# Attention and FFN in one kernel: x loaded into eight tiles of a pool of five, K made chunk by chunk, GpSimd's clearings moved

## The chip, the cores and the metric

The kernel runs on one core of a Trainium2 chip. A core has five engines with an instruction stream each: TensorE (PE: matrix products, its weight loads are shown apart as PEld), VectorE (DVE), ScalarE (ACT), GpSimd (POOL) and SyncE (SP, which here only issues DMAs). Each engine works through its own stream in order and waits on semaphores for the others. The metric is the time of one execution on the device in microseconds (us), lower is better.

## The reference

One token sequence x of 2048 x 512 goes two ways, and a gate mixes them. Way A is attention with 32 heads of 16 numbers, where all heads share one K and one V (multi-query). Way B is a feed-forward layer of width 1792 with SiLU.

```python
g = sigmoid((x * gate_w).sum(-1, keepdims=True))
q = (x @ wq) as 32 heads of 16;  k = x @ wk;  v = x @ wv      # wk, wv: 512 x 16
p = softmax(q @ k.T * 16 ** -0.5)                              # 32 x 2048 x 2048
a = (p @ v, heads side by side) @ wo
b = silu(x @ w1) @ w2                                          # 512 -> 1792 -> 512
out = g * a + (1 - g) * b
```

All is in float32. The kernel gets that precision from 16-bit parts: an operand is split into a high part and the rest, and a product is three matmuls (high x high, high x rest, rest x high).

## The kernel before

**Prologue (`first_pass`, L432 to L567).** It brings x in, turns it over and makes the first operands of the attention, before the first score.

- `loads` (L301) issues on SP's queue eight DMAs of 256 tokens of x, into four tiles of 512 tokens (a chunk), each with its own buffer. The loads of `wqr` (two of wq's four column blocks) stand behind the second DMA of x. The two first pieces of w1 (`raw`) follow on the same queue. wk, wv and the gate's weights come over ACT's queue.
- `T(c, t)` (L328, L331) turns 128 tokens of chunk c on PE (four transposes into a PSUM buffer `pt`, of which there are four). `split` (L121 to L124) takes the high half out on ACT and the rest on DVE, into `xs`. A buffer is free for the next T when DVE is through.
- `wkv` holds wk, wv and the gate's weights side by side. GpSimd gathers it, and `split` makes its two halves `wkvs` (ACT, then DVE).
- `W` (L485) makes wq's halves, on ACT and GpSimd, for two of the four blocks of 128 rows at a time. `Q(kt)` (L502) is a fourth of the product that gives q for the first 512 tokens.
- `K(t)` (L493, L498) is 48 matmuls of 128 columns: for tokens 128 t to 128 t + 127 of **each of the four chunks**, one chunk in each group of 32 partitions. So it needs x of all four chunks. Three K's write `pk`, the fourth another bank `mi`.
- From K come `kh` (the halves of K, on ACT L525 and L530, on DVE L536) and a bound on K's size (`absmax` L523, the minimum against a mask `mxa` L524, the product `prep` L532, `kv_`, `kab` L534). From q come `qs_` and `qa`; `q_bound` (L423) multiplies `qa` by `kab` and gives the shift `s1`, `place` (L348) puts K's first chunk into `KT`, and two groups of matmuls (L554, L558) put q and the shifts into `qb`, the operand of the first scores.
- `cleared(VP, VF)` and `cleared(nus, sc)` (L217) are GpSimd's clearings of V's two buffers, some constants and the second `qb`. The first stands ahead of the gathering of `wkv`, the second behind W(2).

**Main phase (`attention`, L785).** 16 rounds (4 chunks of queries x 4 blocks of 8 heads), each of 32 steps of 64 keys. A step has two score groups (`S`, L1140, 8 matmuls each), two exponentials of 128 x 1024 on ACT (L1146), and its share of P times V (`pv`, L1157, L1166). That share comes in one of two kinds. The whole kind multiplies float32 P by float32 V in one go (8 matmuls `P,VF`). The split kind multiplies P's upper 16 bits by V (part A, `P,VP`) and then P's rest (part B, `L,VP` or `raw,VP`), which DVE has to make first with two subtractions (L1152). The FFN and the projections are fed in as passes (L826): a pass is 4 matmuls, or 8 where two outputs share the array. V itself is made in `begin` (L1172, L1190) while the first scores run.

The order of all this is not found at run time. A planner (`advance`, L1466) steps through PE, ACT and DVE with fixed lengths for every piece of work (`PASS`, `WHOLE`, `EXP`, `LOW` at L30 and L31) and writes each engine's stream in the order that comes out. `decide` (L1309) picks the kind of a step by the time that DVE has left, and `pe_next` (L1370) the next piece on PE.

**End (L1489 to L1520).** Behind the last score PE finishes P times V of the last steps and the last FFN product (`pm<-xs,w1s`). Its tanh (ACT L857), the SiLU (DVE L860), a cast by DMA (POOL L870) and a subtraction (DVE L874) give the last `H`, and 24 matmuls of full width (L830), four last projections (L1518) and the stores close the kernel.

## Time and profile before

| what | us |
|---|---|
| median of 3 runs (lowest, highest) | 1043.51 (1042.72, 1044.07) |
| the profiled execution | 1041.77 |
| its span | 1040.0 |
| first score on PE, first exponential on ACT | 27.14, 27.94 |
| last score on PE | 1013.17 |
| last tanh on ACT | 1018.35 |

The span is what the hardware profiler recorded between the first and the last instruction; 1.8 us of the execution lie around it. In the lines of the profile a row is start, length, engine, line, operation, output<-inputs, count, and in brackets the idle time ahead of it with what ended it. "x48" are 48 instructions that overlap in a row's length. A matmul of float32 makes two records.

### The profile page before, as it was taken

The numbers are of one execution on the slowest core, as the hardware profiler recorded it, in microseconds if no ns is written. First come the engines' busy times: TensorE is split into PE (matmuls) and PEld (weight loads), VectorE is DVE, ScalarE is ACT, GpSimd is POOL, SyncE is SP. The second block draws the span as 40 slices with busy tenths as digits, with TensorE's granted clock in tenths as the row PEclk, the third lists the DMA queues.
The fourth block names the chain that finished last, engine by engine and source line by source line (L and its number), as shares of the span: only waits on it lengthen the run. The fifth ranks groups of instructions, "written<-read, shape, count | busy, mean of one in ns | idle before, by whom it ended". The sixth has DMA issues, their size and how long they took to land.

```text
span 1040.0 us, 63947 instructions
## 1 busy us (share of the span) xinstructions
PE 1012.4 (97%) x30021; PEld 559.1 (54%) x30021; DVE 927.5 (89%) x1197; ACT 993.7 (96%) x1109; POOL 62.4 (6%) x141
## 2 busy tenths in 40 slices
PE   8999999999999999999999999999999999999996
PEld 6335555555555555565555555555555555555552
DVE  7778887779999999999999998999899989999984
ACT  5999999999999999999999999999999999999990
POOL 5001111110000000000000000000000000000000
PEclk9999999999999999999999999999999999999998
DMA  5123221311010121111101021110110021110001
GB/s 206 43 81 73 80 65 50 80 44 30 14 32 12 39 50 20 30 19 31 18 14 30 10 70 24 28 22 14 46 25 14 10 63 21 25 19 14 9 4 49
DMA packets 28091, 39.77 MB, mean 38 GB/s; under 512 B 5689, under 2 KB 19370, under 8 KB 27818
## 3 DMA queue, kind: packets, MB, share of 16 engines
q0 software_dynamic: 10656, 15.73, 7.3%
q1 hardware_dynamic: 16442, 19.27, 6.0%
q8 instruction: 237, 3.88, 1.6%
q10 hardware_dynamic: 720, 0.59, 0.2%
q14 instruction: 36, 0.29, 0.1%
HBM read 19.98 MB, written 8.25 MB: 27 GB/s over the span
## 4 chain that ended last, share of the span: by engine, by line
PE 55%; ACT 33%; DVE 5%; issue 5%; DMA 1%; SPq 0%; ACTq 0%; DVEq 0%
ACT P L1146 31%; PE pm L826 20%; PE pv L1166 17%; PE S L1140 14%; ACT e L857 2%; DVE L L1152 2%; DVE e L860 1%; DVE raw L1152 1%; PE pm L830 1%; PE S L830 1%; DMA xn<-in_A_x_dram 1%; PE pt L331 1%; DVE acc L807 0%; DVE T L1081 0%; DMA H<-e 0%
## 5 line engine op out<-in xcount | busy, mean ns | idle before, releaser
L1146 ACT ACTIVATE P<-S 128x1024 f32<-128x1024 f32 x1024 | 960.3, 1068 | 9.4 <-PE pv L1166 3.3
L1140 PE MATMUL S<-qb,KT 50*32 50x512 f16 x8192 | 444.2, 379 | 10.6 <-ACT P L1146 8.9
L1152 DVE TENSOR_TENSOR L<-P 128x1024 f16<-128x1024 f32 x318 | 379.5, 1217 | 31.1 <-ACT P L1146 30.3
L1140 PEld LDWEIGHTS <-KT 50*32 50x32 f16 x8192 | 200.1, 89 | 250.1 <-issue 162.7
L826 PE MATMUL pm<-xs,w1s 64*32 64x512 f16 x5376 | 305.6, 375 | 0.7 <-DVE e L860 0.3
L826 PE MATMUL pm<-w2s,H 64*32 64x512 f16 x5184 | 293.6, 375 | 1.2 <-DVE e L860 0.7
L1166 PE MATMUL pv<-P,VF 64*32 64x512 f32 x4224 | 284.0, 589 | 0.0
L1152 DVE TENSOR_TENSOR raw<-P 128x1024 f16<-128x1024 f32 x178 | 212.4, 1216 | 5.8 <-ACT P L1146 5.5
L826 PEld LDWEIGHTS <-w1s 64*32 64x32 f16 x5376 | 132.0, 92 | 54.2 <-issue 9.9
L826 PEld LDWEIGHTS <-H 64*32 64x32 f16 x5184 | 127.3, 93 | 48.6 <-issue 10.1
L1166 PE MATMUL pv<-P,VP 64*32 64x512 bf16 x1984 | 112.4, 386 | 0.0
L1166 PEld LDWEIGHTS pv<-P,VF 64*32 64x32 f32 x4224 | 83.0, 106 | 25.7 <-issue 3.8
L1166 PEld LDWEIGHTS <-VP 64*32 64x32 f16 x3968 | 71.0, 92 | 35.9 <-issue 8.9
L1166 PE MATMUL pv<-L,VP 64*32 64x512 f16 x1272 | 86.9, 376 | 0.1
L826 PE MATMUL pm<-xs,wqs 64*32 64x512 f16 x1152 | 86.0, 375 | 0.7 <-DVE e L860 0.7
L870 POOL DMA_DIRECT2D H<-e x56 | 29.8, 532 | 798.8 <-DVE e L860 757.5
L826 PE MATMUL pm<-wo_s,O 64*32 64x512 f16 x1440 | 66.9, 375 | 0.1
L1166 PE MATMUL pv<-raw,VP 64*32 64x512 f16 x712 | 55.8, 376 | 0.0
L860 DVE SCALAR_TENSOR_TENSOR e<-e,pm 128x512 f32<-128x512 f32 x56 | 38.3, 684 | 11.0 <-ACT e L857 10.7
L807 DVE SCALAR_TENSOR_TENSOR acc<-pm,g,acc 128x512 f32<-128x512 f32 x48 | 35.7, 746 | 9.0 <-PE pm L826 8.1
L826 PEld LDWEIGHTS <-wqs 64*32 64x32 f16 x1152 | 37.3, 92 | 9.4 <-issue 2.6
L874 DVE TENSOR_TENSOR H<-e,H 128x512 f16<-128x512 f32 x56 | 38.2, 682 | 3.7 <-DMA H<-e 3.7
(202 smaller groups left out, 491.3 us busy)
## 6 DMA issues: line engine op xcount, KB each, us to landing
H<-e POOLq DMA_DIRECT2D x56, 128.0 KB, 2.3
raw<-in_B_w_dram POOLq DMA_DIRECT2D x24, 256.0 KB, 3.0
qb<-qd SPq DMA_DIRECT2D x180, 32.0 KB
xn<-in_A_x_dram SPq DMA_DIRECT2D x8, 512.0 KB
out_dram<-acc SPq DMA_DIRECT2D x14, 256.0 KB
qd<-qx SPq DMA_DIRECT2D x13, 256.0 KB
raw<-in_A_wo_dram POOLq DMA_DIRECT2D x4, 256.0 KB, 3.0
qb<-sh SPq DMA_DIRECT2D x60, 2.0 KB
```

Source lines behind the costliest of these rows:

```text
L331: nc.tensor.transpose(pt[:, kt], xn[c].rearrange("p t (d k) -> p t k d", k=KD)[:, t, kt], ident)
L807: nc.vector.scalar_tensor_tensor(a, po, gate[:, m:m + 1], a, op0=OP.mult, op1=OP.add)
L826: nc.tensor.matmul(self.bank[32 * m:32 * m + 32], l(i, rows, 32 * m), r(j, rows), start=first, stop=last)
L830: nc.tensor.matmul(self.bank, l(i, slice(0, 128), 0, 128), r(j, slice(0, 128)), start=first, stop=last)
L857: nc.scalar.activation(e, o.bank, AF.Tanh, scale=t_scale)
L860: nc.vector.scalar_tensor_tensor(e, e, 1.0, o.bank, op0=OP.add, op1=OP.mult)
L870: nc.gpsimd.dma_start(H[:, 0], e)
L874: nc.vector.tensor_tensor(H[:, 1], e, H[:, 0], op=OP.subtract)
L1140: nc.tensor.matmul(sc[32 * m:32 * m + 32, f], KT[b:b + 50, k0:k0 + 32], qtile[i][b:b + 50, m // 2, j], start=True, stop=True)
L1146: nc.scalar.activation(probs[s][:, 2 * j:2 * j + 2], banks.pop(p), AF.Exp, scale=scale_of(*rounds[steps[s][0]]))
L1152: nc.vector.tensor_tensor(lows[s, j], probs[s][:, js], upper(probs[s])[:, js], op=OP.subtract)
L1166: nc.tensor.matmul(pvs[i][h][32 * j:32 * j + 32], a[r], b[r], start=k == 0 and n != "B", stop=k == NK - 1 and n != "A")
```

## The change

x comes into eight tiles of 256 tokens out of a pool of five buffers, so that the sixth, seventh and eighth load wait until PE has turned the first, second and third tile. The load of `wqr` moves behind the fourth tile of x. `W(n)` works on 128 columns of all four row blocks, so that Q needs only W(0).

`K(c)` now takes **one chunk's** four groups of 128 tokens, one in each group of partitions, and so can run as soon as that chunk is turned. The keys then stand in another order in `KT`, and V and the gate are made in the same order (L1190, L1207: the operand is read as four blocks of 128 columns). The halves of `wkv` are made early by ACT and GpSimd and not by DVE. All of GpSimd's clearings stand behind W(1). Behind K the order on ACT, DVE and PE changes, and K's first chunk is put into `KT` by DVE and not by ACT.

In the planner the constant `WHOLE` = 0.866 is gone. `HALF` = 0.435 is there, and the whole kind (now "W") counts as 2 x 0.435 = 0.870. The two half kinds "N" and "M" that `pv` knows are given to no step.

```diff
-PASS, PASS_S, PASS_P, WHOLE, LATE = 0.217, 0.219, 0.231, 0.866, 0.23
+PASS, PASS_S, PASS_P, HALF, LATE = 0.217, 0.219, 0.231, 0.435, 0.23
...
-    def loads(sb, q_cols, wq_at=NCH - 1):
+    def loads(sb, q_cols, wq_at=NCH - 1, ahead=2 * NCH):
...
-        for c in range(NCH):
-            t_ = sb.tile([128, 4, D], F32, name=f"xn{c}")
-            if c == wq_at:
+        for n in range(2 * NCH):
+            t_ = sb.tile([128, 2, D], F32, name="xn", bufs=ahead)
+            nc.sync.dma_start(t_, x[n * 256:n * 256 + 256].rearrange("(t p) d -> p t d", p=128))
+            xn.append(t_)
+            if n == 2 * wq_at + 1:
                 nc.sync.dma_start(wqr, by_row(wq)[:, :, :q_cols])
-            for a in range(2):
-                nc.sync.dma_start(t_[:, 2 * a:2 * a + 2], x[c * 512 + a * 256:c * 512 + a * 256 + 256].rearrange("(t p) d -> p t d", p=128))
-            xn.append(t_)
...
-            nc.tensor.transpose(pt[:, kt], xn[c].rearrange("p t (d k) -> p t k d", k=KD)[:, t, kt], ident)
+            nc.tensor.transpose(pt[:, kt], xn[2 * c + t // 2].rearrange("p t (d k) -> p t k d", k=KD)[:, t % 2, kt], ident)
...
-            xn, wqr, wkv, gather = loads(sb, 256, 1)
+            xn, wqr, wkv, gather = loads(sb, 256, 1, 5)
...
-            def W(kt):
-                nc.scalar.activation(wqs[:, 0, kt:kt + 2, 0:256], wqr[:, kt:kt + 2], AF.Copy, scale=SQ)
-                nc.gpsimd.tensor_scalar(wqr[:, kt:kt + 2], wqr[:, kt:kt + 2], SQ, None, op0=OP.mult)
-                nc.gpsimd.tensor_tensor(wqs[:, 1, kt:kt + 2, 0:256], wqr[:, kt:kt + 2], wqs[:, 0, kt:kt + 2, 0:256], op=OP.subtract)
+            def W(n):
+                b = slice(128 * n, 128 * n + 128)
+                nc.scalar.activation(wqs[:, 0, :, b], wqr[:, :, b], AF.Copy, scale=SQ)
+                nc.gpsimd.tensor_scalar(wqr[:, :, b], wqr[:, :, b], SQ, None, op0=OP.mult)
+                nc.gpsimd.tensor_tensor(wqs[:, 1, :, b], wqr[:, :, b], wqs[:, 0, :, b], op=OP.subtract)
...
-            def K(*ts):
-                for t in ts:
+            def K(c):
+                out = pk[c // 3][:, c % 3 * 128:c % 3 * 128 + 128]
+                for n, (i, j) in enumerate(((0, 0), (1, 0), (0, 1))):
                     for kt in range(KD):
-                        for n, (i, j) in enumerate(PARTS):
-                            for c in range(NCH):
-                                nc.tensor.matmul(pk[t // 3][32 * c:32 * c + 32, t % 3 * 128:t % 3 * 128 + 128], wkvs[:, i, kt, 0:32],
-                                                 xs[:, j, kt, c * 512 + t * 128:c * 512 + t * 128 + 128],
-                                                 start=kt + n == 0, stop=kt == KD - 1 and n == 2)
+                        for g in range(4):
+                            nc.tensor.matmul(out[32 * g:32 * g + 32], wkvs[:, i, kt, 0:32],
+                                             xs[:, j, kt, c * 512 + g * 128:c * 512 + g * 128 + 128],
+                                             start=kt + n == 0, stop=kt == KD - 1 and n == 2)
...
+            first, last = slice(0, 384), slice(384, 512)
+
+            def largest(n, bank):
+                absmax(mx[:, n:n + 1], bank)
+                nc.vector.tensor_scalar(mxa[:, n], m_k, mx[:, n:n + 1], None, op0=OP.min)
+
+            def rest(b, r):
+                nc.vector.scalar_tensor_tensor(kh[1][:, r], b, k_to, kh[0][:, r], op0=OP.mult, op1=OP.subtract)
...
             place_masks()
             row_masks()
-            cleared(VP, VF)
             gather()
-            T(0, 0, 1, 2, 3)
+            nc.gpsimd.tensor_scalar(wkv, wkv, SKV, None, op0=OP.mult)
+            T(0, 0, 1)
+            nc.scalar.activation(wkvs[:, 0], wkv, AF.Copy)
+            nc.gpsimd.tensor_tensor(wkvs[:, 1], wkv, wkvs[:, 0], op=OP.subtract)
+            T(0, 2, 3)
             T(1, 0, 1)
             W(0)
             T(1, 2, 3)
-            W(2)
+            T(2, 0)
+            K(0)
+            T(2, 1)
+            W(1)
+            cleared(VP, VF)
             cleared(nus, sc)
-            T(2, 0)
-            split(wkvs[:, 0], wkvs[:, 1], wkv, SKV)
-            T(2, 1, 2)
+            T(2, 2, 3)
+            K(1)
+            T(3, 0, 1, 2)
+            K(2)
+            nc.scalar.activation(kh[0][:, first], pk[0][:, first], AF.Copy, scale=k_to)
+            T(3, 3)
+            largest(0, pk[0][:, first])
             Q(0)
-            T(2, 3)
-            T(3, 0, 1, 2, 3)
             Q(1)
-            K(0, 1, 2)
-            absmax(mx[:, 0:1], pk[0][:, 0:384])
-            nc.vector.tensor_scalar(mxa[:, 0], m_k, mx[:, 0:1], None, op0=OP.min)
-            nc.scalar.activation(kh[0][:, 0:384], pk[0][:, 0:384], AF.Copy, scale=k_to)
             K(3)
             Q(2)
-            absmax(mx[:, 1:2], pk[1][:, 0:128])
-            nc.vector.tensor_scalar(mxa[:, 1], m_k, mx[:, 1:2], None, op0=OP.min)
-            nc.scalar.activation(kh[0][:, 384:512], pk[1][:, 0:128], AF.Copy, scale=k_to)
+            Q(3)
+            nc.scalar.activation(kh[0][:, last], pk[1][:, 0:128], AF.Copy, scale=k_to)
+            nc.scalar.activation(qs_[:, 0], pq, AF.Copy, scale=qsc)
+            largest(1, pk[1][:, 0:128])
             prep = misc()
             nc.tensor.matmul(prep[:, 0:8], flat(sel_k), flat(mxa), start=True, stop=True)
-            nc.vector.tensor_reduce(kv_, prep[:, 0:8], axis=AX.X, op=OP.max)
-            nc.vector.tensor_scalar(kab, hmask, kv_, k_to * 2.0 ** -10 * (1 + 2.0 ** -9), op0=OP.mult, op1=OP.mult)
-            for b, r in enumerate((slice(0, 384), slice(384, 512))):
-                nc.vector.scalar_tensor_tensor(kh[1][:, r], pk[b][:, 0:r.stop - r.start], k_to, kh[0][:, r], op0=OP.mult, op1=OP.subtract)
-            Q(3)
-            pieces_.step(by_scalar=True)
-            qs_ = wk_.tile([128, 2, 512], F16, name="qs_")
-            qa = wk_.tile([128, 512], F16, name="qa")
-            nc.scalar.activation(qs_[:, 0], pq, AF.Copy, scale=qsc)
-            nc.vector.tensor_scalar(qa.bitcast(U16), qs_[:, 0].bitcast(U16), 0x7FFF, None, op0=OP.bitwise_and)
-            nc.vector.scalar_tensor_tensor(qs_[:, 1], pq, qsc, qs_[:, 0], op0=OP.mult, op1=OP.subtract)
-            place(misc(), 0, True)
-            pu = misc()
-            q_bound(pu, qa)
-            s1 = wk_.tile([64, 512], F16, name="s1")
-            nc.scalar.activation(s1, pu[0:64], AF.Copy, scale=-2.0 ** 10 / ONE, bias=SHIFT * LAM / ONE)
...
-            for n in range(2):
+
...
+            spread(0)
+            rest(pk[0][:, first], first)
+            nc.vector.tensor_reduce(kv_, prep[:, 0:8], axis=AX.X, op=OP.max)
+            nc.vector.tensor_scalar(kab, hmask, kv_, k_to * 2.0 ** -10 * (1 + 2.0 ** -9), op0=OP.mult, op1=OP.mult)
+            rest(pk[1][:, 0:128], last)
+            nc.vector.tensor_scalar(qa.bitcast(U16), qs_[:, 0].bitcast(U16), 0x7FFF, None, op0=OP.bitwise_and)
+            pu = misc()
+            q_bound(pu, qa)
+            pieces_.step(by_scalar=True)
+            nc.scalar.activation(s1, pu[0:64], AF.Copy, scale=-2.0 ** 10 / ONE, bias=SHIFT * LAM / ONE)
+            nc.vector.scalar_tensor_tensor(qs_[:, 1], pq, qsc, qs_[:, 0], op0=OP.mult, op1=OP.subtract)
+            place(misc(), 0, False)()
+            spread(1)
...
-            if k == 0:
+            if k == 0 and n != "M":
                 pvs[i] = [pO.tile([128, 512], F32, name=f"pv{h}") for h in range(2)]
-            a = VF[:, k] if n == "N" else VP[:, k]
+            a = VF[:, k] if n in "WNM" else VP[:, k]
+            q = slice(0, 256) if n == "N" else slice(256, 512) if n == "M" else slice(0, 512)
             for j in range(4):
-                b = upper(probs[s])[:, j] if n == "A" else probs[s][:, j] if n == "N" else lows[s, j // 2][:, j % 2]
+                b = upper(probs[s])[:, j] if n == "A" else probs[s][:, j] if n in "WNM" else lows[s, j // 2][:, j % 2]
                 for h, r in enumerate((lo, hi_)):
-                    nc.tensor.matmul(pvs[i][h][32 * j:32 * j + 32], a[r], b[r], start=k == 0 and n != "B", stop=k == NK - 1 and n != "A")
-            if n != "A":
+                    nc.tensor.matmul(pvs[i][h][32 * j:32 * j + 32, q], a[r], b[r, q], start=k == 0 and n != "B", stop=k == NK - 1 and n != "A")
+            if n in "BMW":
                 probs.pop(s)
...
-                        nc.tensor.matmul(v[32 * c:32 * c + 32], wkvs[:, i, kt, 32:64], xs[:, j, kt, c * 512:c * 512 + 512],
+                        nc.tensor.matmul(v[32 * c:32 * c + 32], wkvs[:, i, kt, 32:64], xs[:, j, kt].rearrange("p (c g n) -> p g c n", c=NCH, g=4)[:, c],
...
-                        z = gz.rearrange("p (c u o) -> p u c o", c=NCH, o=1)[h, 2 * a:2 * a + 2]
+                        z = gz.rearrange("p (u c o) -> p u c o", c=NCH, o=1)[h, 2 * a:2 * a + 2]
...
-                    how[s] = "N"
+                    how[s] = "W"
...
-                if r is not None and (left_of[s][0] != "N" or max(r, now["PE"]) <= most):
+                if r is not None and (left_of[s][0] in "AB" or max(r, now["PE"]) <= most):
...
-            length = {"A": PASS_P, "B": PASS, "N": WHOLE}[n]
+            length = {"A": PASS_P, "B": PASS, "N": HALF, "M": HALF, "W": 2 * HALF}[n]
...
-            x = pv_next(end - PASS_S - LATE - WHOLE + SLACK if p < 2 * len(steps) else 1e9)
+            x = pv_next(end - PASS_S - LATE - 2 * HALF + SLACK if p < 2 * len(steps) else 1e9)
```

The last of it moves the streams of the main phase. They are alike up to the 60th score group. Then they differ in detail: 261 steps are of the whole kind (264 before) and 251 of the split kind (248 before), and DVE gets 502 subtractions L1152 (496 before).

On PE, in the prologue, the products for K (`pk`, `mi`, from `xs` and the weights in `wo_s`) stand behind the last transposes (`pt`) and behind two of the four Q's (`pq`). Before:

```order
L442 MATMUL mi<-ident 128x128 x15
L331 MATMUL pt<-ident,xn_187 128x128 x16
L331 MATMUL pt<-ident,xn_190 128x128 x16
L331 MATMUL pt<-ident,xn_194 128x128 x12
L132 MATMUL pq<-xs,wqs 128x512
...
L331 MATMUL pt<-ident,xn_197 128x128 x16
...
L498 MATMUL pk<-xs,wo_s 32x128
```

And after, where each row of L498 stands for the first of 48:

```order
L441 MATMUL mi<-ident 128x128 x15
L330 MATMUL pt<-ident,xn 128x128 x36
L498 MATMUL pk<-xs,wo_s 32x128
...
L330 MATMUL pt<-ident,xn 128x128 x12
...
L330 MATMUL pt<-ident,xn 128x128 x4
L132 MATMUL pq<-xs,wqs 128x512
...
L498 MATMUL mi<-xs,wo_s 32x128
```

K(0) moved up behind the ninth T, K(1) and K(2) behind the twelfth and the fifteenth. All four Q's stand behind the last T, two ahead of K(3) and two behind it.

On GpSimd (POOL) in the prologue the clearings of `VP` and `VF` stand ahead of the gathering of `wkv`. Before:

```order
L461 MEMSET sels__215 64x512
L219 MEMSET VP 128x1024
L219 MEMSET VF 128x1024
L322 COPY wkv<-wkr 128x4x16
L324 COPY wkv<-gwr 128x4
L487 TENSOR_SCALAR wqr<-wqr 128x512
L488 TENSOR_TENSOR wqs<-wqr,wqs 128x2x256
L219 MEMSET nus 128x48
```

After:

```order
L460 MEMSET sels__219 64x512
L321 COPY wkv<-wkr 128x4x16
L323 COPY wkv<-gwr 128x4
L521 TENSOR_SCALAR wkv<-wkv 128x256
L524 TENSOR_TENSOR wo_s<-wkv,wo_s 128x256
L487 TENSOR_SCALAR wqr<-wqr 128x4x128
L488 TENSOR_TENSOR wqs<-wqr,wqs 128x4x128
L219 MEMSET VP 128x1024
L219 MEMSET VF 128x1024
L219 MEMSET nus 128x48
```

The two clearings moved from the front of the stream to behind both W's, right ahead of the constants `nus` and the clearing of `qb`, and the two rows on `wkv` are new on this engine.

On PE, at the end of the main phase, from the last score group (`S`) on, with the FFN's passes (`pm`) and P times V (`pv0`). Before:

```order
L1140 MATMUL S_33004<-qb1_84,KT_60 32x512
L826 MATMUL pm_32807<-xs_66,w1s_67 32x512
L1166 MATMUL pv0_31190<-P_32859,VF_63 32x512
...
L1166 MATMUL pv0_31190<-P_32931,VF_63 32x512
...
L1166 MATMUL pv0_31190<-P_32994,VF_63 32x512
...
L830 MATMUL S_33097<-w2s_68,H_31485 128x512
```

After:

```order
L1158 MATMUL S_32936<-qb1_84,KT_60 32x512
L844 MATMUL pm_32750<-w2s_68,H_29766 32x512
...
L1185 MATMUL pv0_31207<-P_32870,VF_63 32x512
...
L1185 MATMUL pv0_31207<-L_32868,VP_61 32x512
...
L1185 MATMUL pv0_31207<-P_32932,VF_63 32x512
...
L844 MATMUL pm_32750<-w2s_68,H_30023 32x512
...
L844 MATMUL pm_32945<-xs_66,w1s_67 32x512
L848 MATMUL S_33136<-w2s_68,H_31603 128x512
```

Before, three whole steps and 10 passes of the FFN stand between the last score group and the 24 closing matmuls. After, it is two whole steps, one part B and 24 passes. In the whole first pass the passes number 1697 before and 1703 after.

12 lines of the change are left out of this document (8 added, 4 removed).

## The prediction

> **What bounds the kernel now.** I read the page first (its shares of busy time and the chain that ended last), then stretches of the main phase, and then the chain and the single rows of the first 28 us and the last 30.
>
> ```profile
> span 1040.0 us, 63947 instructions
> ...
> PE 1012.4 (97%) x30021; PEld 559.1 (54%) x30021; DVE 927.5 (89%) x1197; ACT 993.7 (96%) x1109; POOL 62.4 (6%) x141
> ...
> PE 55%; ACT 33%; DVE 5%; issue 5%; DMA 1%; SPq 0%; ACTq 0%; DVEq 0%
> ...
> L1146 ACT ACTIVATE P<-S 128x1024 f32<-128x1024 f32 x1024 | 960.3, 1068 | 9.4 <-PE pv L1166 3.3
> ...
> L1152 DVE TENSOR_TENSOR L<-P 128x1024 f16<-128x1024 f32 x318 | 379.5, 1217 | 31.1 <-ACT P L1146 30.3
> ```
> ```profile
> 28.00:128.00 100.00, 99.13 (x2313) 44.15 (x2317) 80.25 (x163) 97.22 (x105) 11.40 (x20) 1.00 0.26 71
> ...
> 328.00:428.00 100.00, 97.93 (x3012) 55.89 (x3004) 94.75 (x109) 99.73 (x112) 3.19 (x6) 1.00 0.13 32
> ```
>
> The second fence is busy time by stretch of 100 us (PE, PEld, DVE, ACT, POOL, clock, DMA). ACT is busy 97 to 99.7% of the main phase, PE nearly as much, DVE 95%. Over the whole phase the exponentials waited visibly for only 9.4 us. So three engines are close to each other, and the main phase gets shorter only if all of them get less. The prologue stands ahead of all that: what it saves is saved.
>
> The prologue by its chain, from the first DMA to the first score:
>
> ```profile
> 3.16 7.52 DMA xn<-in_A_x_dram
> ...
> 10.82 4.12 PE pt L331 x20
> ...
> 15.59 2.66 PE pt L331 x20
> ...
> 18.90 2.26 PE pk L498 x144
> 21.16 0.67 PE mi L498 x48
> ...
> 23.37 0.23 PE pq L134
> ...
> 27.14 0.88 PE S L1140 x12
> ```
>
> Up to 10.7 it is the arrival of x, from then to 23.6 PE alone, then 3.5 us of handing over to the first score at 27.14. PE had time to spare earlier, and for a stretch it ran at half clock (rows by 1 us; the next to last columns are clock, DMA share, GB/s):
>
> ```profile
> 6.41 1.23 PE L331 MATMUL pt<-ident,xn 128*128 128x128 f32 x8 [0.30 <-DMA xn<-in_A_x_dram]
> 9.48 1.70 PE L331 MATMUL pt<-ident,xn 128*128 128x128 f32 x9 [1.84 <-DMA xn<-in_A_x_dram]
> ```
> ```profile
> 11.00:12.00 1.00, 1.00 (x7) 1.00 (x7) 1.00 (x2) 1.00 (x3) 0.07 (x1) 0.59 1.05 393
> 12.00:13.00 1.00, 1.00 (x6) 1.00 (x5) 0.75 (x2) 0.74 (x2) 1.00 (x1) 0.50 1.03 381
> ```
>
> **The change, part by part.** *Loads.* There are still eight DMAs of x and one of wqr, 512 KB each. At 390 GB/s one takes 1.35 us; the fifth landed at 10.7, so the sixth lands at 12.05 and the ninth, the last of x, at 16.1, in both kernels. The sixth to eighth tile now wait for PE's transposes of the first three, of which the second's end at 7.6 (6.41 + 1.23) and the third's at about 9; queued behind them on SP are only the two raw pieces of w1, first read by ACT behind q. The queue holds 512 KB pieces until 12 by then, so this wait costs nothing. Its cover ends if the third tile is turned later than about 11.
>
> *K by chunks.* The counts stay: 64 transposes, 192 small matmuls, 12 for Q. From the landing of the fifth tile of x (12.05) PE has 8 T's, 4 K's and 4 Q's to do. A T is 4 x 2.66 / 20 = 0.53 us, a K (2.26 + 0.67) / 4 = 0.73, a Q 3 x 0.215 = 0.65: 4.2 + 2.9 + 2.6 = 9.8. PE would be through with Q at 21.8, where it was at 23.6: **-1.8**. Behind the last tile (16.1) there are at least two T's, two K's and four Q's, 5.1 us, so 21.2 (-2.4) is the earliest. If the half clock comes back between 12.05 and 14.7, where a T took 4.12 / 5 = 0.82, it costs 2.65 x (1 - 0.53 / 0.82) = 0.9. ACT and DVE keep up: DVE's rests of x go at 4.26 / 7 = 0.61 each.
>
> ```profile
> 15.57 4.26 DVE L124 SCALAR_TENSOR_TENSOR xs<-pt,xs 128x512 f16<-128x512 f32 x7
> ...
> 11.21 0.63 ACT L486 ACTIVATE wqs<-wqr 128x512 f16<-128x512 f32 x1
> ```
>
> W(0) now waits on ACT for wqr (10.7 in place of about 8), with the outputs of two T's queued behind it. That is a delay of about one us at 11.3, with four `pt` buffers as cover, and the next tile comes at 12.05: nothing.
>
> The Trainium skill, page "TensorE: Matmul & The Clock Gate", section "Part 1: The HAM clock gate (the "warmup" mystery)", says that the half clock comes after an idle window of about 3.4 us. The trace does not agree: here it came with no wait longer than 1.84 us. By the page the new prologue, with shorter waits, would keep the full clock and the -1.8; by the row it may lose 0.9 of it.
>
> *Clearings later.* GpSimd's clearings ran beside DVE's masks, and one mask of 128 x 32 was held:
>
> ```profile
> 3.42 0.21 DVE L259 TENSOR_SCALAR kone<-rm 128x1 f32<-128x1 f32 x1
> 3.55 2.11 DVE L260 TENSOR_SCALAR hj<-hj,pm 128x32 f32<-128x32 f32 x1
> 5.69 0.32 DVE L261 TENSOR_SCALAR hm<-hj 128x32 f32<-128x32 f32 x1
> ...
> 23.16 0.24 DVE L534 TENSOR_SCALAR kab<-hmask,kv__207 128x32 f16<-128x32 f32 x1
> ```
> ```profile
> 3.78 0.94 POOL L219 MEMSET VP<- 128x1024 f16 x1
> 4.67 0.94 POOL L219 MEMSET VF<- 128x1024 f32 x1
> ...
> 14.76 1.49 POOL L487 TENSOR_SCALAR wqr<-wqr 128x512 f32<-128x512 f32 x1
> 16.34 1.16 POOL L488 TENSOR_TENSOR wqs<-wqr,wqs 128x512 f16<-128x512 f32 x1
> 17.44 0.14 POOL L219 MEMSET nus<- 128x48 f32 x1
> ...
> 18.33 1.80 POOL L230 MEMSET qb<- 128x2048 f16 x1
> ```
>
> L260 took 2.11 us, until the clearing of VF was done, where the like L261 took 0.32. That wait (1.8) goes, but DVE was only late for x's rests, not the last. In exchange the clearings come late: W(1) stands on ACT behind T(2,1), which PE ends at 12.05 + 0.53 + 0.73 + 0.53 = 13.8; ACT takes 0.6 for it and 0.6 for W, so GpSimd begins at about 15.1, needs 1.5 + 1.2, then 0.9 + 0.9 for VP and VF, 0.2, 0.9 for the constants and 1.8 for `qb`: busy to about 22.5. `kab`, of L260's form, is due at 22.3. It is held until 22.5, and the shift, the rows and the first score come 0.4 later. Handing over is otherwise as long as before: 27.14 - 23.6 = 3.5. First score: 21.8 + 3.5 + 0.4 = 25.7, **-1.4**. If `mxa` (128 x 4, due at 20.5) is held as long as L260, that is until 22.5, then `absmax`, `mxa`, `prep`, `kv_` and `kab` follow and the score comes at 26.7 (-0.4). I take `mxa` as free, by L259 (128 x 1, 0.21 us beside a clearing). Ends: -2.4 and, with the half clock and `mxa` held, +0.7.
>
> The Trainium skill, page "SBUF — State Buffer", section "Who interferes with whom", says that the one of DVE and GpSimd that issues second waits for the other's whole instruction. By the page `mxa` would wait for one short clearing at most, and the sum would stay at -1.4; the trace's L260 sat through more than one clearing, which would make it -0.4.
>
> *V's keys, wkv's halves, KT by DVE.* The same matmuls with the same columns; the 48 small changes of place go with what is costed above: 0. Their cover is PE's other work beside the first scores.
>
> *The planner's constant.* It moves 2.4 us of PE work to the end. Lengths on PE, from one stretch of the main phase: a whole step is 302.15 to 303.01 = 0.87 us, a pass (303.88 to 304.75) / 4 = 0.217, as a part B:
>
> ```profile
> 302.15 1.06 PE L1166 MATMUL pv<-P,VF 64*32 64x512 f32 x16
> 303.01 0.41 PE L1140 MATMUL S<-qb,KT 50*32 50x512 f16 x8
> ...
> 303.88 1.06 PE L826 MATMUL pm<-xs,w1s 64*32 64x512 f16 x32
> 304.75 0.41 PE L1140 MATMUL S<-qb,KT 50*32 50x512 f16 x8
> ```
> ```profile
> 1013.17 0.39 PE L1140 MATMUL S<-qb,KT 50*32 50x512 f16 x4
> ...
> 1016.40 1.90 PE L826 MATMUL pm<-xs,w1s 64*32 64x512 f16 x32
> ```
> ```profile
> 1018.35 0.60 ACT L857 ACTIVATE e<-pm 128x512 f32<-128x512 f32 x1 [3.69 <-PE pm L826]
> ```
>
> Behind the last score there were 10 passes and 3 whole steps, 2.2 + 2.6 = 4.8, and the last tanh began 5.2 after that score, so PE's order sets it. Now there are 24 passes, 2 whole steps and a part B, 5.2 + 1.7 + 0.2 = 7.2: **+2.4** up to the last tanh, and behind it all is as before. Ahead of the last score PE has 8 passes and two whole steps fewer, three parts A and two parts B more: -1.7 - 1.7 + 0.7 + 0.4 = -2.4. So PE's total is the same. If PE set the pace all along, the main phase would give the 2.4 back; if ACT does, it gives nothing, since ACT's 1024 exponentials and 56 tanhs stay. I take 0, by ACT's 99.7% and its 9.4 us of waits. DVE gets six subtractions more, 6 x 1.22 = 7.3 us at 95% busy: from 0 (it fits the 5% left) to +7.3. I take 0, since ACT waited for DVE in no row of the page.
>
> The sum: -1.4 + 2.4 + 0 = +1.0 on the profiled 1041.77 (span 1040.0), so 1042.8. That execution lies 1.7 under the median of 1043.5, which gives **1044.5**. One can tell 0.2% (2.1 us) from no change, so this is no change.
>
> **The rivals.**
> - *PE sets the pace (faster).* For it: PE has 55% of the chain and ACT 33%. Then the 2.4 comes back: -1.4, and with the prologue at its best -2.4: 1041.1. Against it: ACT's busy rows.
> - *DVE gets the bound (slower).* In the split steps PE's part B waits for both subtractions, P's four buffers come free later, and ACT waits for those. Place: the middle, where DVE is 95% busy. Price: up to 7.3, so up to 1051.8; half of it gives 1048.1. It decides once 1.1 of the 7.3 shows. For it: DVE's row. Against: 31 us in which the subtractions waited for ACT, not ACT for them.
> - *The prologue does not get shorter.* Half clock and `mxa` behind the clearings: first score at 27.8, +0.7 in place of -1.4: 1046.6, slower.
>
> **How the numbers follow.** No change has 0.45, PE as the bound 0.22, DVE as the bound 0.23, the prologue that gains nothing 0.10. Faster by over 0.2% 0.22, within it 0.45, slower 0.33. The range goes from the first rival (1041.1) to half the second's price (1048.1); the likeliest case alone is 1042.1 (the 2.4 given back) to 1045.5 (`mxa` held).
>
> **What would show it.** First score at 25.7 (25 to 27), K(0) at about 12.6, no half clock from 11 to 15; `kab` ending with the clearing of `qb`; last tanh 7.6 behind the last score in place of 5.2; first to last score 986.0 as before, or 2.4 less if PE sets the pace, or more with new waits on L1152 if DVE does. I would be wrong above all if the new order of the main phase makes waits of its own, since three nearly full engines leave no cover, or if the closing matmuls ran at another clock.

## The result, and the profile after

The changed kernel took 1048.55 us (median of 5 runs, 1047.24 to 1050.94), the kernel before 1043.51 beside it: a ratio of 1.0053, 95% interval 1.0038 to 1.0068. So it is 5.0 us slower, and the forecast of no change (1044.5) was wrong. The profiled execution spans 1046.1 us where that of before spanned 1040.0.

The page of the kernel after, its busy row, the engines' shares of the chain that ended last, and two of the costliest groups:

```profile
span 1046.1 us, 63965 instructions
...
PE 1016.0 (97%) x30021; PEld 557.6 (53%) x30021; DVE 934.3 (89%) x1203; ACT 992.2 (95%) x1108; POOL 64.0 (6%) x143
...
PE 43%; ACT 30%; issue 18%; DVE 6%; DMA 2%; POOL 0%; ACTq 0%; DVEq 0%; POOLq 0%
...
L1164 ACT ACTIVATE P<-S 128x1024 f32<-128x1024 f32 x1024 | 959.7, 1074 | 13.4 <-PE pv L1185 6.3
...
L875 ACT ACTIVATE e<-pm 128x512 f32<-128x512 f32 x56 | 36.6, 654 | 6.3 <-PE pm L844 6.3
```

L1164 is the line of the exponentials (L1146 before), L1158 that of the scores, L1185 P times V, L875 the tanhs. ACT is busy about as long as before (992.2 us beside 993.7). What grew is what it waits: ahead of the exponentials 13.4 us in place of 9.4, ahead of the last tanh 6.3 in place of 3.7. The same from ACT's waits of the kernel after (us in total, times, longest), and behind it the first of these lines before:

```profile
ACT P L1164 <- PE pv L1185: 6.3, 9, 1.5
ACT e L875 <- PE pm L844: 6.3, 1, 6.3
ACT P L1164 <- PE S L1158: 3.9, 11, 0.9
```
```profile
ACT P L1146 <- PE pv L1166: 3.3, 5, 0.7
```

An exponential that waits for `pv` waits for one of P's four buffers. Before, these waits were 3.3 us in 5 places.

Three marks by which the whole can be split, after, from PE's and ACT's timelines:

```profile
28.52 1.31 PE L1158 MATMUL S<-qb,KT 50*32 50x512 f16 x16
```
```profile
1017.61 0.41 PE L1158 MATMUL S<-qb,KT 50*32 50x512 f16 x8
```
```profile
1025.50 0.60 ACT L875 ACTIVATE e<-pm 128x512 f32<-128x512 f32 x1 [6.27 <-PE pm L844]
```

The first score at 28.52 (27.14 before) is +1.4; from there to the last score 989.1 (986.0) is +3.1; from there to the last tanh 7.9 (5.2) is +2.7; from there to the end 20.6 (21.7) is -1.1. Together 6.1, the difference of the two spans. One mark is not quite the same in both: the 1013.17 of before is the second half of the last score group, which was pulled apart there and began earlier:

```profile
1012.78 0.41 PE L1140 MATMUL S<-qb,KT 50*32 50x512 f16 x4
```

From the start of the last group the two differences in the middle are +3.4 and +2.3 in place of +3.1 and +2.7. These are single executions; how far one can be trusted is seen below.

The prologue after, by its chain (first 29 us):

```profile
3.54 8.47 DMA xn<-in_A_x_dram
...
12.15 1.10 PE pt L330 x4
13.25 1.40 PE pk L498 x25
14.65 2.02 PE pt L330 x12
...
22.41 1.92 DVE mxa L509
...
25.30 0.24 DVE kab L563
...
28.52 0.88 PE S L1158 x12
```

PE's wait for x, the granted clock by single microseconds (the next to last columns: clock, DMA share, GB/s), and what GpSimd did while `mxa` took 1.92 us:

```profile
12.15 1.10 PE L330 MATMUL pt<-ident,xn 128*128 128x128 f32 x4 [1.32 <-DMA xn<-in_A_x_dram]
```
```profile
11.00:12.00 1.00, 0.00 (x0) 0.00 (x0) 0.39 (x2) 1.00 (x3) 0.60 (x1) 1.00 1.05 387
12.00:13.00 1.00, 0.85 (x4) 0.73 (x4) 1.00 (x2) 0.29 (x1) 0.92 (x2) 0.61 1.06 389
13.00:14.00 1.00, 1.00 (x34) 0.82 (x36) 0.20 (x2) 0.60 (x1) 1.00 (x1) 0.50 1.05 385
14.00:15.00 1.00, 1.00 (x30) 0.80 (x19) 0.61 (x1) 0.00 (x0) 0.14 (x1) 0.50 1.06 391
```
```profile
22.46 0.10 POOL L229 MEMSET nus<- 128x1 f32 x1
22.50 1.80 POOL L230 MEMSET qb<- 128x2048 f16 x1
```

So the third rival happened in this execution: half clock from 12 to 16 us, and `mxa` held from 22.41 to 24.33, until the clearing of `qb` (22.50 + 1.80) was done. PE was through with Q at 24.0, before `mxa`, so `mxa` and what hangs on it (`kab`, the shift, the rows) set the first score.

### The profile page after: what moved, and what is told of

It reads as the page before. It is cut to its first block, busy times and chain, and to the rows that moved or that the text cites. A ratio compares the mean times of both kernels' runs of the same rounds, so it can differ in the third digit from the quotient of the medians.

```text
span 1046.1 us, 63965 instructions
## 1 busy us (share of the span) xinstructions
PE 1016.0 (97%) x30021; PEld 557.6 (53%) x30021; DVE 934.3 (89%) x1203; ACT 992.2 (95%) x1108; POOL 64.0 (6%) x143
## 4 chain that ended last, share of the span: by engine, by line
PE 43%; ACT 30%; issue 18%; DVE 6%; DMA 2%; POOL 0%; ACTq 0%; DVEq 0%; POOLq 0%
ACT P L1164 28%; PE pm L844 15%; PE pv L1185 14%; PE S L1158 11%; DVE L L1170 2%; ACT e L875 2%; DVE raw L1170 2%; DVE e L878 1%; PE pm L848 1%; DMA xn<-in_A_x_dram 1%; PE S L848 1%; DMA H<-e 1%; DVE acc L825 1%; PE pt L330 1%; POOL H L888 0%
## 5 line engine op out<-in xcount | busy, mean ns | idle before, releaser
L1164 ACT ACTIVATE P<-S 128x1024 f32<-128x1024 f32 x1024 | 959.7, 1074 | 13.4 <-PE pv L1185 6.3
L1158 PE MATMUL S<-qb,KT 50*32 50x512 f16 x8192 | 444.1, 380 | 11.5 <-ACT P L1164 9.2
L1170 DVE TENSOR_TENSOR L<-P 128x1024 f16<-128x1024 f32 x322 | 383.4, 1217 | 29.1 <-ACT P L1164 28.3
L1158 PEld LDWEIGHTS <-KT 50*32 50x32 f16 x8192 | 200.0, 89 | 259.0 <-issue 173.8
L844 PE MATMUL pm<-xs,w1s 64*32 64x512 f16 x5376 | 300.3, 375 | 1.3 <-DVE e L878 1.0
L1185 PE MATMUL pv<-P,VF 64*32 64x512 f32 x4176 | 279.3, 589 | 0.4 <-issue 0.4
L1170 DVE TENSOR_TENSOR raw<-P 128x1024 f16<-128x1024 f32 x180 | 214.8, 1216 | 5.7 <-ACT P L1164 5.5
L1185 PE MATMUL pv<-P,VP 64*32 64x512 bf16 x2008 | 113.5, 386 | 0.0
L1185 PEld LDWEIGHTS <-VP 64*32 64x32 f16 x4016 | 73.0, 92 | 39.8 <-issue 13.3
L1185 PEld LDWEIGHTS pv<-P,VF 64*32 64x32 f32 x4176 | 80.3, 106 | 23.4 <-issue 3.3
L1185 PE MATMUL pv<-L,VP 64*32 64x512 f16 x1288 | 87.5, 375 | 0.0
L1185 PE MATMUL pv<-raw,VP 64*32 64x512 f16 x720 | 55.9, 376 | 0.1
L878 DVE SCALAR_TENSOR_TENSOR e<-e,pm 128x512 f32<-128x512 f32 x56 | 38.3, 685 | 15.0 <-ACT e L875 14.9
L875 ACT ACTIVATE e<-pm 128x512 f32<-128x512 f32 x56 | 36.6, 654 | 6.3 <-PE pm L844 6.3
```

The lines of the kernel that those rows point to most:

```text
L844: nc.tensor.matmul(self.bank[32 * m:32 * m + 32], l(i, rows, 32 * m), r(j, rows), start=first, stop=last)
L875: nc.scalar.activation(e, o.bank, AF.Tanh, scale=t_scale)
L878: nc.vector.scalar_tensor_tensor(e, e, 1.0, o.bank, op0=OP.add, op1=OP.mult)
L1158: nc.tensor.matmul(sc[32 * m:32 * m + 32, f], KT[b:b + 50, k0:k0 + 32], qtile[i][b:b + 50, m // 2, j], start=True, stop=True)
L1164: nc.scalar.activation(probs[s][:, 2 * j:2 * j + 2], banks.pop(p), AF.Exp, scale=scale_of(*rounds[steps[s][0]]))
L1170: nc.vector.tensor_tensor(lows[s, j], probs[s][:, js], upper(probs[s])[:, js], op=OP.subtract)
```

## The experiments

Theory: most of the 5 us comes of the planner's constant alone, which gives the whole main phase another order; the prologue gains nothing because of the half clock and of `mxa`. Rival: the prologue's edits reach into the main phase (V's keys read in groups of 128, everything 1.4 us later), and the constant is harmless.

**The constant alone (e1_constant), the prologue alone (e2_prologue).** In the kernel before:

```diff
-PASS, PASS_S, PASS_P, WHOLE, LATE = 0.217, 0.219, 0.231, 0.866, 0.23
+PASS, PASS_S, PASS_P, WHOLE, LATE = 0.217, 0.219, 0.231, 0.870, 0.23
```

> The kernel before, with nothing changed but the planner's constant for a whole pass of the probabilities, 0.866 to 0.870 (what twice 0.435 is). My theory after the result: the constant alone makes the main phase 3.1 us longer and the tail 2.7 us longer, because the planner's order is another one. Then the first score stands at 27.1 as before, first to last score takes 989 instead of 986, last score to last tanh 7.9 instead of 5.2, and the time is 4.5 to 6 us above before, near 1048.5. The rival: the main phase lost its 3.1 us to the prologue's edits that reach into it (V's keys read in groups of 128, the first score later). Then first to last score takes 986, and only the tail's 2.7 us or nothing of it is seen: 1043.5 to 1046.2.

In the kernel after:

```diff
-PASS, PASS_S, PASS_P, HALF, LATE = 0.217, 0.219, 0.231, 0.435, 0.23
+PASS, PASS_S, PASS_P, HALF, LATE = 0.217, 0.219, 0.231, 0.433, 0.23
```

> The changed kernel with HALF 0.433 instead of 0.435, so that the planner counts 0.866 for a whole pass as it did before: the changed prologue and V's order without the changed constant. My theory: first to last score 986 and last score to last tanh 5.2 as before, the first score at 28.5 as in the changed kernel, the time 1.4 us above before: 1044.9. The rival, that the prologue's edits cost the main phase its time: first to last score 989, 1047.5 to 1048.5.

Measured: the constant alone is 1.0040 of before (1.0026 to 1.0054), +4.2 us; first score 27.3, first to last score 988.8, tail 7.9. The prologue alone is 1.0011 (1.0002 to 1.0020), +1.1 us; first score 27.0, 986.6, 5.2. ACT's waits with the constant alone, and with the prologue alone:

```profile
ACT P L1146 <- PE pv L1166: 7.0, 10, 1.5
ACT e L857 <- PE pm L826: 6.3, 1, 6.3
```
```profile
ACT e L875 <- PE pm L844: 3.7, 1, 3.7
ACT P L1164 <- PE pv L1185: 3.3, 5, 0.7
```

The fingerprint of the changed main phase, 6 to 7 us for `pv` and 6.3 for the last tanh, goes with the constant and not with the prologue. The theory holds and the rival falls. Of the prologue's first score I had expected 28.5; it came at 27.0, without the half clock.

**Which use of the constant, and which value (c_length, c_margin, c431, c437).** The constant stands in two places: as the length that is booked on PE's planned clock, and as a margin ahead of the next scores. Each run puts 0.866 back in one of them, in the kernel after:

```diff
 # c_length: the margin is 0.866 again, the booked length stays 0.870
-            x = pv_next(end - PASS_S - LATE - 2 * HALF + SLACK if p < 2 * len(steps) else 1e9)
+            x = pv_next(end - PASS_S - LATE - 0.866 + SLACK if p < 2 * len(steps) else 1e9)
 # c_margin: the booked length is 0.866 again, the margin stays 0.870
-            length = {"A": PASS_P, "B": PASS, "N": HALF, "M": HALF, "W": 2 * HALF}[n]
+            length = {"A": PASS_P, "B": PASS, "N": HALF, "M": HALF, "W": 0.866}[n]
```

> The changed kernel (HALF 0.435) with 0.866 put back in one of the constant's two places, the time by which a whole pass must start to be through before the next scores; the length that is booked on TensorE's planned clock stays 0.870. If the booked length is what shifts the order, this run is as slow as the changed kernel: first to last score 989, tail 7.9, 1046 to 1049. If it is the margin, it is as fast as the one with 0.433: 986.6, 5.2, 1042.5 to 1044.5.

> The other half: the booked length is 0.866 again, the margin ahead of the next scores stays at 0.870. If the margin shifts the order: 989, 7.9, 1046 to 1049. If the booked length: 986.6, 5.2, 1042.5 to 1044.5. If both runs come out slow, neither place is the cause by itself and any change of the planned order costs some us.

The other two keep both places and change the value, 0.862 and 0.874 for a whole pass:

```diff
-PASS, PASS_S, PASS_P, HALF, LATE = 0.217, 0.219, 0.231, 0.435, 0.23
 # c431
+PASS, PASS_S, PASS_P, HALF, LATE = 0.217, 0.219, 0.231, 0.431, 0.23
 # c437
+PASS, PASS_S, PASS_P, HALF, LATE = 0.217, 0.219, 0.231, 0.437, 0.23
```

> The changed kernel with HALF 0.431: the planner counts 0.862 for a whole pass, as far below 0.866 as the change's 0.870 is above it. The first theory: the main phase's 3 us and the tail's 2.7 us come of the pass being counted longer, so a shorter count gives no more than the kernel before: first to last score 985 to 987, tail 5.2, 1042 to 1043.5. The rival: what the change lost is luck, any other order near the one that 0.866 gives is worse; first to last score 988 or more, the time 1044.5 to 1048. In either case the prologue is the changed kernel's; its first score tells whether 28.5 is the rule (half clock from 12 to 16 us) or 27.0 as with HALF 0.433.

> The changed kernel with HALF 0.437: 0.874 for a whole pass, further up than the change's 0.870. The first theory (the longer count costs the time): first to last score 989 or more, tail 7.9 or more, 1046.5 to 1050. The rival (luck of the order): anything from 986 to 990 and no growth with the constant; since this order has as many subtractions on VectorE as the one of 0.866 (six fewer than that of 0.870), it is expected near it: 1042.5 to 1045.

Measured: c_length 1.0044 (1.0027 to 1.0060), c_margin 1.0006 (0.9997 to 1.0016). The booked length is what costs. c431 is 1.0035 (1.0023 to 1.0048), c437 1.0074 (1.0057 to 1.0091). So a step down costs as well as a step up, and neither account fits as I gave it: in both, first to last score is *shorter* than in the first profile of the kernel before, by 0.9 and 2.1 us (0.5 and 1.7 from the start of the last group; both are less than one execution differs from another, as seen below), and the tail longer, by 2.9 and 9.7. The last tanh of c437, from ACT's timeline:

```profile
1027.47 0.60 ACT L875 ACTIVATE e<-pm 128x512 f32<-128x512 f32 x1 [13.31 <-PE pm L844]
```

The orders differ in how many of the FFN's matmuls (`pm`) they leave behind the last score: 44 with 0.866, 148 with 0.862 and 0.870, 268 with 0.874. (Four of each count are not the FFN's but the last projections, which write `pm` too; the 40 and 144 that are left are the 10 and 24 passes named above the prediction.)

**The waits at round changes (t_first).** A place at which the orders part, DVE in the kernel after, and ACT there:

```profile
342.65 1.22 DVE L1170 TENSOR_TENSOR raw<-P 128x1024 f16<-128x1024 f32 x1 [0.96 <-ACT P L1164]
343.90 0.75 DVE L825 SCALAR_TENSOR_TENSOR acc<-pm,gg,acc 128x512 f32<-128x512 f32 x1
344.57 1.22 DVE L1170 TENSOR_TENSOR L<-P 128x1024 f16<-128x1024 f32 x1
345.70 1.31 DVE L1099 STREAM_TRANSPOSE T<-pv 128x512 f32<-128x512 f32 x2
```
```profile
348.73 1.94 ACT L1164 ACTIVATE P<-S 128x1024 f32<-128x1024 f32 x2 [1.53 <-PE pv L1185]
```

The transposes that empty the `pv` banks at a round's end stand behind two subtractions and the adding of a projection to the output (`acc`, with the gate `gg`); the next round's P times V starts late, P's buffers come free late, and ACT stands still for 1.53 us. The same wait of 1.5 us stands at this place in e1_constant, c_length and c437, all with a booked length of 0.870 or more, and in none of the others with the planner's old rules. To take it away, one rule of the planner, in the kernel after:

```diff
-            task(t, lambda: t if idle[0] else None, 1.25, first)
+            task(t - 60, lambda: t if idle[0] else None, 1.25, first, True)
```

> The changed kernel, constant 0.435 and all, with one rule of the planner added: the two transposes that empty the pv banks at a round's end go ahead of every other task of VectorE and have room kept for them. My theory: the changed order's 3 us in the main phase are ScalarE's waits at round changes, because a subtraction and a step of the second model stand ahead of these transposes; then the waits of the exponentials for pv fall from 6.3 us to 3 or less, first to last score goes from 989.1 to 986 or below, and the time falls by 2 to 4 us under the changed kernel's. The rival: the waits move elsewhere (a later L, a longer tail), and the time stays within 1 us of the changed kernel's.

Measured: 1.0055 (1.0041 to 1.0068), the same as the changed kernel. ACT's waits:

```profile
ACT e L875 <- PE pm L844: 13.3, 1, 13.3
ACT P L1164 <- PE S L1158: 4.0, 12, 0.6
ACT P L1164 <- PE pv L1185: 0.6, 1, 0.6
```

The waits for `pv` went from 6.3 to 0.6 and the main phase from 989.1 to 984.9, both as my theory had it; and the tail grew from 7.9 to 15.2, with 332 `pm` matmuls behind the last score. The rival is right about the time. The rule made another whole order, so the run does not price these waits by themselves; it shows that an order without them is no faster.

**The clearings taken forward (e4_clearings).** The kernel with HALF 0.433, and

```diff
+            cleared(nus, sc)
             T(0, 2, 3)
             T(1, 0, 1)
             W(0)
+            cleared(VP, VF)
...
             W(1)
-            cleared(VP, VF)
-            cleared(nus, sc)
```

> The run with HALF 0.433, and GpSimd's clearings taken forward: those of nus and sc right behind the split of the weights, those of VP and VF behind W(0), none behind W(1), so that GpSimd is through with qb's clearing before VectorE makes mxa. My theory: mxa's 1.92 us are the wait for that clearing, so mxa takes 0.2 us, and what is late next is Q's last matmul; the first score goes from 28.5 to 26.8, 1.7 us earlier, and the time to 1043.2. The rival: mxa's 1.92 us hide the wait for Q, which ends late anyway; the first score goes no further than 28.0 and the time stays at 1044.5 or above.

Measured: `mxa` took 0.23 us both times, and the first score came at 26.64, where e2_prologue with `mxa` held for 1.58 us has it at 27.04.

```profile
L509 DVE TENSOR_SCALAR mxa<-m_k,mx x2: 229/230/231, 21.3 to 22.2; 128x4 f32<-128x4 f32 x2
```
```profile
L509 DVE TENSOR_SCALAR mxa<-m_k,mx x2: 229/904/1578, 21.3 to 22.9; 128x4 f32<-128x4 f32 x2
```

(First the clearings forward, then e2_prologue.) So `mxa` does wait for `qb`'s clearing. Without that wait, Q's last matmul at 22.66 and the copies behind it set the first score, at 26.6, as expected. The gain is 0.4 us beside a prologue at full clock. In the time it does not show: 1.0008 of before (0.9999 to 1.0017), 1.0011 without.

**PE kept busy through the wait for x (e5_busy_wait).** Further:

```diff
             T(1, 2, 3)
+            for _ in range(9):
+                nc.tensor.transpose(pq[:, 0:128], ident, ident)
             T(2, 0)
```

> The run with the clearings taken forward, and nine transposes of the identity into a bank that is not in use yet, set before the transpose that waits 1.3 us for the third chunk of x, so that TensorE works through that wait. My theory: the half clock of 12 to 16 us comes from that idle time; without it the granted clock there is 0.98 or above, K(0) and the four transposes behind it are about 1 us shorter, and the first score comes 0.8 to 1.2 us earlier than without the nine: 25.8, 1042.2. The rival: the half clock comes of something else, or x's arrival bounds the stretch all the same, and the first score stays within 0.3 us of 26.8; the nine transposes could also end after x's arrival, which would cost up to 0.5 us.

Measured: 1.0004 (0.9995 to 1.0013), first score at 27.70, 1.1 us later than without, which neither the theory nor the rival had. The clock stayed at 1.00 from 11 to 16 us, but so it did in e2_prologue and e4_clearings, where PE waited 0.3 us for x at this place (and 1.35 for DVE just ahead). The nine ended at 13.03, and K(0) began at 13.51 where it had begun at 12.66 without them. Of these 0.85 us 0.40 were there already ahead of the nine (the transposes before them began at 10.70 in place of 10.30), so the nine cost about 0.45. On the clock this run settles nothing.

**K(0) ahead of the transpose that waits for x (k_first), and both ideas together (k_and_t).** To the run with the clearings forward:

```diff
-            T(2, 0)
             K(0)
+            T(2, 0)
```

> The run with HALF 0.433 and the clearings taken forward, with K(0) ahead of the transpose that waits for the third chunk of x, in place of behind it. My theory: K(0)'s 0.78 us fall into the wait for x, the rest of the prologue follows TensorE without a gap, and the first score comes 0.7 us earlier than 26.6: 25.9; the time 1041.8, level with before. The rival: the transposes or the scalings behind them set the stretch anyway: 26.4 to 26.8, no change of the time.

> The two together with HALF 0.433: K(0) first, the clearings forward, and the transposes at a round's end ahead of all. If the round changes' waits cost the kernel before time as well (3.3 us there), first to last score falls to 984 to 985 and the time to 1040, 1.5 us under before. The rival, the luck of the order: anything from 1040 to 1046.

Measured: k_first 0.9992 (0.9983 to 1.0001), first score at 26.80. The rival is right on the score: K(0) began at 11.66 in place of 12.66 and half a microsecond of that was still there at K(2), but then PE stood 0.96 us for nothing that the profile shows. It is the best of the changed kernels, 0.6% under the changed one, and not to be told from the kernel before. k_and_t, k_first with t_first's rule added, is 1.0106 (1.0090 to 1.0121), the slowest of all, with the shortest main phase but for one. The main phase, 984.3, came as the theory had it; the time, 11 us above before, is outside both the theory and the rival. Its waits on ACT:

```profile
ACT e L875 <- PE pm L844: 17.6, 1, 17.6
...
ACT P L1164 <- PE pv L1185: 0.6, 1, 0.6
```

**The kernel before once more (before_again).**

> The kernel before, unchanged, for a second profile of it. If its prologue and its main phase come out as in the first (first score 27.1 with the half clock from 11 to 15 us, first to last score 986.0), the 0.6 to 1.3 us that the runs with its order and the changed prologue show more in the main phase belong to the change. If the main phase comes out at 986.5 to 987.5, they are the scatter of one execution to another.

Measured: 1.0004 (0.9995 to 1.0014). Its first score is at 27.50 and its first to last score 989.5, 3.4 us more than in the first profile, with the same order of instructions, and so outside both of the values that I had set for it. Three waits for a score are new, in ACT's timeline:

```profile
405.81 3.77 ACT L1146 ACTIVATE P<-S 128x1024 f32<-128x1024 f32 x4 [0.61 <-PE S L1140]
...
650.43 4.80 ACT L1146 ACTIVATE P<-S 128x1024 f32<-128x1024 f32 x5 [1.29 <-PE S L1140]
...
899.93 1.02 ACT L1146 ACTIVATE P<-S 128x1024 f32<-128x1024 f32 x1 [0.76 <-PE S L1140]
```

So the scatter of one execution's main phase is as large as the +3.1 that I read off two profiles. What bears the reading is the medians, and the two waits that stay with an order: for `pv` 3.3 or 3.5 us in all seven profiles with 0.866 as the booked length and the old rules, 6.3, 7.0 and 6.3 in the three with 0.870, and the last tanh's 3.7 and 6.3.

All together (us; "pm left" is the number of `pm` matmuls behind the last score in PE's order):

| kernel | ratio to before | first score | first to last score | to last tanh | ACT waits: pv, last tanh | pm left |
|---|---|---|---|---|---|---|
| before, before_again | 1, 1.0004 | 27.1, 27.5 | 986.0, 989.5 | 5.2, 5.2 | 3.3, 3.7 (3.5, 3.7) | 44 |
| after | 1.0053 | 28.5 | 989.1 | 7.9 | 6.3, 6.3 | 148 |
| e1_constant | 1.0040 | 27.3 | 988.8 | 7.9 | 7.0, 6.3 | 148 |
| e2_prologue | 1.0011 | 27.0 | 986.6 | 5.2 | 3.3, 3.7 | 44 |
| e4_clearings | 1.0008 | 26.6 | 987.4 | 5.2 | 3.3, 3.7 | 44 |
| e5_busy_wait | 1.0004 | 27.7 | 987.3 | 5.2 | 3.3, 3.7 | 44 |
| k_first | 0.9992 | 26.8 | 987.2 | 5.2 | 3.3, 3.7 | 44 |
| c_margin | 1.0006 | 27.5 | 987.4 | 5.2 | 3.3, 3.7 | 44 |
| c_length | 1.0044 | 27.2 | 987.8 | 7.9 | 6.3, 6.3 | 148 |
| c431 | 1.0035 | 27.2 | 985.2 | 8.1 | 3.1, 6.3 | 148 |
| c437 | 1.0074 | 28.6 | 983.9 | 14.9 | 3.7, 13.3 | 268 |
| t_first | 1.0055 | 27.1 | 984.9 | 15.2 | 0.6, 13.3 | 332 |
| k_and_t | 1.0106 | 26.7 | 984.3 | 19.8 | 0.6, 17.6 | 436 |

In the rows with 44 the last score is counted from the second half of its group, as before; from the group's start, as in the other rows, their main phase is 0.4 shorter and their tail 0.4 longer.

Every kernel that leaves 44 `pm` matmuls is within 0.11% of before, whatever its prologue; every one that leaves more is slower by 0.35% or more, whatever its main phase.

PE's work and its waits can be read apart in the stretch from the first score to the last tanh. Here it is for before, after and k_and_t (length of the stretch; busy time of PE, PEld, DVE, ACT and POOL; clock, DMA share, GB/s):

```profile
27.14:1018.35 991.21, 977.55 (x29689) 537.34 (x29689) 897.16 (x1124) 978.16 (x1082) 48.23 (x89) 1.00 0.14 33
```
```profile
28.52:1025.50 996.98, 981.56 (x29689) 536.13 (x29689) 905.98 (x1134) 977.32 (x1082) 48.23 (x89) 1.00 0.14 33
```
```profile
26.71:1030.81 1004.10, 983.78 (x29689) 533.55 (x29689) 910.29 (x1137) 978.82 (x1081) 48.30 (x89) 1.00 0.14 33
```

All fourteen profiles have 29689 matmul records in it, and ACT is busy for 976.8 to 978.8 us. PE's busy time is 977.6 to 979.6 in the seven with 44 left and 981.1 to 982.1 in the three with 0.870; in c431, c437, t_first and k_and_t it is 977.8, 980.7, 981.7 and 983.8. PE's idle time is 13.7 to 15.0 in the seven, 14.5 to 15.4 in the three, and 15.5, 18.2, 18.4 and 20.3 in the last four. So a slow order keeps PE busy for longer over the same number of matmuls, or leaves it idle for longer, or both; with 0.870 it is mostly the first, +3.0 of +3.9 on average. That is what outweighs a shorter main phase.

What stays open: why PE is busy for longer over as many matmuls. More passes with one output in place of two is a candidate (1703 passes in place of 1697), but by the planner's own lengths the three whole steps fewer make up for these; small waits that hide in the overlap of the matmuls are another. Neither was measured.

## Why the prediction was wrong, point by point

- **Two terms of the sum failed: the main phase, taken as 0, and the prologue, -1.4.** By the times of the runs that part the change, the constant cost 4.2 us where the sum had 2.4 for it, and the prologue cost 1.1 (0.6 in c_margin, which has the same prologue and also leaves 44) where the sum had a gain of 1.4. So the prologue is the larger miss, by 2.0 to 2.5 us against 1.8.
- **The main phase.** I let ACT's 99.7% and its 9.4 us of waits stand for a main phase that an exchange of a few passes can't lengthen. The constant alone (e1_constant) took the waits for `pv` from 3.3 to 7.0. Its 988.8 beside 986.0 is no evidence by itself, since before_again has 989.5; from the first score to the start of the last group the three profiles with 0.870 take 988.5 on average and the seven that leave 44 take 987.0, which is +1.6, and with the tail's +2.3 that comes near the 4.2. "So PE's total is the same" was right by the planner's lengths and wrong by the traces: PE was busy for 981.1 to 982.1 us in place of 977.6 to 979.6. My range for this term, -2.4 to +7.3, held it. That the new order might make "waits of its own, since three nearly full engines leave no cover" I had named as what would make me wrong, and gave it no price in the sum.
- **The rival on DVE** had the place and the carrier right (the middle of the main phase, P's buffers come free late, ACT waits for them) and its half price, 1048.1, is nearest to the result. That is luck, since its mechanism was not what ran. DVE is at 89% in both kernels, and c437, with 496 subtractions as before, has the same wait of 1.5 us; it comes where the transposes at a round's end stand behind subtractions and an addition to the output. And the 1.4 us that its sum took off for the prologue did not come.
- **The rival on PE's pace** forecast that what the main phase gives up at the end is given back. It was not: no run with 148 or more `pm` left is faster than before. But c437, t_first and k_and_t show the other half of it: a main phase shorter by 0.7 to 1.7 us than in the first profile of before (from the start of the last group) was paid for in the tail, with 9 to 14.
- **The tail, +2.4**, worked out from the passes behind the last score, measured +2.3 from the start of the last group (+2.7 by the rows), and the same with the constant alone. Right. "Behind it all is as before" was 1.1 us off in the profile of after and 0.1 in that of e1_constant; before_again is 0.9 off, so this is scatter.
- **The prologue, -1.4 (-2.4 to +0.7)**, failed in sign. The first score was to come at 25.7. The seven profiles with the changed prologue as it is have it between 27.0 and 28.6, 27.6 on average, beside 27.1, 27.3 and 27.5 in the three with the old one: +0.3 by the profiles, +1.1 (0.2 to 2.0) by the times. Three steps in it were mis-sized. I took `mxa` as free by L259's row, a 128 x 1 form; the row of L260 was the right one, and `mxa` was held for 1.6 to 1.9 us in each of the seven. And I set the half clock's 0.9 aside: it came in two of the seven, after and c437, which are the two with 28.5 and 28.6. There K(0) took 1.40 and the four transposes ahead of it 1.10, where they take 0.78 and 0.72 at full clock. The third is PE's own work. In e4_clearings, at full clock and with `mxa` at 0.23, the first score still came at 26.64 and not at 25.3 (the 25.7 without the 0.4 for `kab`): from 11.95 PE took 10.9 us up to the end of Q, where I had added up 9.8. The T's took 4.8 in place of 4.2 with 0.3 of idle time between, the K's 3.1 in place of 2.9, the Q's 2.7 in place of 2.6; the handing over took 3.75 in place of 3.5.
- **K(0) at 12.6** was 13.2 in after and 12.7 in e2_prologue. The fifth tile's landing, 12.05, was right: 12.01.
- **L260** was set free by the later clearings as predicted (0.39 us in place of 2.11) and it bought nothing, as predicted.
- **V's keys, wkv's halves, KT by DVE: 0.** With the order of 0.866 and all these edits (e2_prologue to k_first) the times are within 0.11% of before.
- **The sum.** Prologue -1.4 + 2.4 tail + 0 = +1.0 against a measured +5.0. From the two runs that part the change: constant +4.2, prologue +1.1.

## What to carry to other kernels

Where a planner writes out the order of three nearly full engines, a constant of its clock can change the whole program: 0.004 us in one booked length changed the order of a thousand us of work and cost 0.4%, and 0.004 the other way cost nearly as much. Neither direction was free here, so such a constant has to be priced as a new order. Look first at what the new order leaves behind the last step of the bounding chain; here this one number, counted without any run, parted the slow kernels from the others. And price a small DVE instruction that comes beside GpSimd's work by the worst row that ran beside such work, not by the best.

## What the runs showed of the hardware that was not expected

- *After waits of 1.3 us the half clock came in some executions and not in others.* With the old prologue PE waited 1.84, 1.71 and 1.86 us for x, and the half clock followed in all three profiles. With the changed one, in six profiles, it waited 1.31 to 1.33 us, and the half clock followed in two of them (after 1.32, c437 1.31) and not in the four others (c431 1.33):

```profile
12.20 0.72 PE L330 MATMUL pt<-ident,xn 128*128 128x128 f32 x4 [1.33 <-DMA xn<-in_A_x_dram]
```
```profile
13.00:14.00 1.00, 1.00 (x51) 0.90 (x44) 0.57 (x2) 0.55 (x1) 0.99 (x1) 1.00 1.04 385
```

  In four profiles more PE waited 1.32 to 1.35 us for DVE at this time and kept the full clock (e2_prologue, e4_clearings, e5_busy_wait, k_first). Where it came after a wait of 1.3 us, the first score was 1.0 to 1.5 us later. That the wait is its cause was not shown. The Trainium skill, page "TensorE: Matmul & The Clock Gate", section "Part 1: The HAM clock gate (the "warmup" mystery)", gives an idle window of about 3.4 us for it; these traces do not agree.
- *A small DVE instruction was held until GpSimd's clearings were done.* In all seven profiles `mxa` (128 x 4) ended 0.03 us behind the clearing of `qb`; with that clearing gone it took 0.23. In three of them (e2_prologue, c431, t_first) it began within this clearing, in the four others 0.01 to 0.09 us ahead of it, beside the last short ones. L260 (128 x 32) in the kernel before sat through two, from 3.55 to 5.66. The Trainium skill, page "SBUF — State Buffer", section "Who interferes with whom", has the second of the two wait for the other's instruction; `mxa` in the three agrees, L260 sat through more than one.
- *One execution's main phase can be 3.4 us longer than another's of the same program*, with a new wait for a score in three places (0.6, 1.3 and 0.8 us), while the medians of 11 and 21 runs agree within 0.04%.
